# Two Strassen levels instead of one for the last 1024 tokens' products with w_out

## The chip, the cores and the metric

The kernel runs on one core of a Trainium2 chip. The metric is device time in microseconds (us); lower is better. Engines are named as in the profile: PE (matmuls), PEld (weight loads for PE), DVE (vector), ACT (scalar), POOL (GpSimd), SP (its queue issues DMAs here). Each engine works off its own instructions in program order, and waits on semaphores for others.

## The reference

A decayed linear attention over 8 batches, 8 heads, 576 tokens, head size 64, and then a feed-forward block without a non-linearity other than a product:

```
ret = (scores * Dmat) @ v          # scores = q k^T / 8, Dmat = gamma^(i-j) for i >= j
x   = ret as [8*576, 512]
a, b = x @ w1, x @ w2              # 512 -> 1024 each
out = ((a * b) @ w3) @ w_out       # 1024 -> 1024 -> 512
```

All data are fp32. The output has 4608 rows of 512.

## The kernel before

**Merged weights.** `(ab @ w3) @ w_out` is computed as `ab @ (w3 @ w_out)`: the product of the two weights is made once (`w3_mm`, L536) and kept as the tile `w3o`, 1024 x 512. "Products with w_out" are products of `ab` (tokens x 1024) with it. `live["W"]` names the seven forms of it that Strassen's algorithm needs, in Winograd's variant: four quarters `B11`, `B21`, `B22`, `T3` (in `w3o`, the last in place of the fourth quarter) and three sums `T1`, `T2`, `-T4` (tile `wB`). A form is 512 x 256: four chunks of 128 rows on partitions, 256 columns.

**Stages.** Batches go in four pairs. The first pair and the first 64 tokens of each other batch go through single-level code (`up`, L585; `down`, L754). For each of the three other pairs (loop over `s`), 1024 tokens remain: 512 of each of two batches. For them the code does

- the attention, in chunks of 128 tokens (`head`, `tail`), between which the `down` calls of the pair before are laid;
- `up2` (L1039): `x @ w1` and `x @ w2` by two levels of Strassen. For each half `h` of the 1024 features there are seven outer products (order `ORDER` = 1, 2, 6, 5, 3, 7, 4), each of seven inner ones (`INNER` = 1, 5, 6, 2, 7, 3, 4): 14 blocks `k` of 7 products, 98 in all, of 256 columns each;
- products of a and b (`multiply`, L1116) in place in `slab`, which leaves `ab` there;
- `down` (L733): products of two tiles of 128 tokens with `w3o`, one Strassen level, seven products of four matmuls with 256 columns; sums on DVE into `ot`, stores to DRAM from ACT's queue (`store`, L812).

For the pairs `s` = 0 and 1 the four `down` calls are laid between the attention chunks of the next pair. For the last pair (`s` = 2) nothing follows, so four `down` calls stand alone at the end. A call takes 12.09 us.

**The order.** It is written out by hand: each engine gets its instructions in the order in which the Python code issues them. In `up2` a product has a slot number, 7k + 2 x (position in `INNER`), so that two neighbouring blocks interleave (odd and even slots). `at_slot(n, fn)` puts further work behind the product of slot n (the dict `side`).

**Banks and evictions in `up2`.** Each block has two PSUM banks of its own, x and y, and a bank `z` is shared. Product 1 goes to x; ACT copies x to z (L1087); product 2 adds onto z; products 6, 7 and 4 add onto x; 5 and 3 onto y. So product 7 may only begin when the eviction of product 6 has read x, product 4 when that of product 7 has, and so on. Evictions are DVE additions from PSUM into `slab` (L1082; 128x512, or "wide" 128x1024 in outer product 7), ACT copies (L1089), or, for products 2 and mostly 4, an ACT copy into a ring of three buffers (L1081) and a POOL addition from it (L1082 on POOL).

**At the start of `up2`** the token sums are made: T3 and T2 on DVE before it, T1 on DVE behind slot 1, and T4 on POOL, issued behind slot 12, all at L1018 (128x1792). `T4` needs T2 alone. The weight forms of `up2` come from DRAM into four buffers `FB` (`fetch`); `TT` holds T2, T4 and T1. POOL does six `multiply` calls, behind slots 27 to 93; DVE does the other two, right after `up2` and inside the first `down`. In the last `up2`, `ahead` puts one DVE sum of the first `down` (`S3`, L713) behind slot 66.

Of the kernel before, what the change touches and what calls it, by code (L numbers as in the profile page):

```python
# [42 lines left out]
def kernel(  # L43
# [80 lines left out]
    def new(nm, shape, tag=None):  # L124

        if "banks" not in pools:
            return acc.tile(shape, F32, tag="acc", name=nm)
        got = tag or free.pop(0)
        t = pools["banks"].tile(shape, F32, tag=got, name=nm)
        if not tag:  # L130
            held[id(t)] = got, t
        return t

    def done_with(t):
        if id(t) in held:
            free.append(held.pop(id(t))[0])
# [589 lines left out]
    def ahead(x, y, n=3):  # L726
        todo_sums = pair_of(x, y)[2]
        for _ in range(min(n, len(todo_sums))):
            aside.append(todo_sums.pop(0))
# [3 lines left out]
    def down(x, y, then=None, last=False, within=None, hold=False, by_ring=False):  # L733
        a, done, left = pair_of(x, y)
        ahead(x, y)
        while len(done) < 3:
            aside.pop(0)()
        if then:
            ahead(*then)
        ps = {}  # L740
        pool, tag = (F_pool, "ring") if by_ring else ot_pool or (pools["ot"], "ot")
        ot = pool.tile([P, 2, 2, DM // 2], F32, tag=tag, name="ot")

        count = [0]

        def hook():
            count[0] += 1
            if within and count[0] in within:
                within[count[0]]()

        def product(nm, A, B, on=None):
            ps[nm] = ps[on] if on else new("po", [P, DM // 2])
            for f in range(NP):
                nc.tensor.matmul(ps[nm], a[A][:, f // 2, f % 2, :], live["W"][B][:, f, :], start=(f == 0 and not on),  # L754
                                 stop=(f == NP - 1), skip_group_check=True)

        def plus(nm, to, sb):
            nc.vector.tensor_add(ot[:, to[0], to[1]], ps[nm], ot[:, sb[0], sb[1]])  # L758
            if nm != 5:
                done_with(ps[nm])  # L760
            if beside:
                beside.pop(0)()

        def put(m, t, row, half=slice(0, 2)):

            for at, n, r in rows(m, t):
                stores.append((out[r:r + n, half.start * DM // 2:half.stop * DM // 2],
                               ot[at:at + n, row, half].rearrange("p h d -> p (h d)")))
            if not keep_stores:
                store()  # L770

        C11, C12, C21, C22 = (0, 0), (0, 1), (1, 0), (1, 1)
        product(1, "A11", "B11")
        nc.scalar.copy(ot[:, 0, 0], ps[1])  # L774
        hook()
        product(7, "S3", "T3")
        hook()
        product(2, "A12", "B21", on=1)
        nc.vector.tensor_tensor(out=a["S4"], in0=a["A12"], in1=a["S2"], op=ALU.subtract)
        hook()  # L780
        product(6, "S2", "T2")
        plus(6, C12, C11)
        hook()
        nc.scalar.copy(ot[:, 0, 0], ps[2])
        done_with(ps[2])
        plus(7, C21, C12)
        product(5, "S1", "T1")
        plus(5, C22, C21)
        hook()
        product(4, "A22", "-T4")  # L790
        plus(4, C21, C21)
        put(*y, 1)
        if last:
            put(*x, 0, slice(0, 1))
        hook()
        product(3, "S4", "B22", on=5)
        while aside:
            aside.pop(0)()
        plus(3, C12, C12)
        if hold:  # L800
            keep_stores.append(True)
        put(*x, 0, slice(1 if last else 0, 2))
        if hold:
            keep_stores.clear()
        hook()
# [233 lines left out]
    def up2(side, n0):  # L1039

        z = new("upz", [P, 2, NS], "z")
        ring = F_pool.tile([P, 3, 2, NS], F32, tag="ring", name="ring")
        begun_at = {}
        moved = {(1, 1): 3, (12, 5): 98, (12, 6): 100}
        late = {(1, 1): 8}
        slots = sorted((moved.get((k, pos), 7 * k + 2 * pos), k, pos) for k in range(14) for pos in range(7))
        waiting = {}

        def one(slot, k, pos):
            h, j, pr = k // 7, ORDER[k % 7], INNER[pos]  # L1050
            a, b = weights(n0 + k, pr), token_form(j)[:, RHS[pr]]
            if pr == 1:
                begun_at.setdefault(k, [None, None])[0] = new("up", [P, 2, NS])
            elif pr == 5:
                begun_at.setdefault(k, [None, None])[1] = new("up", [P, 2, NS])
            x, y = begun_at[k]
            ps = {1: x, 6: x, 7: x, 4: x, 5: y, 3: y, 2: z}[pr]
            for w in range(2):
                nc.tensor.matmul(ps[:, w, :], a[:, w, :], b, start=(pr in (1, 5) and w == 0), stop=True,  # L1059
                                 skip_group_check=True)  # L1060
            src, dst = TARGET[j]
            S = slab[:, h:h + 2]
            wide = j == 7
            if wide:
                out = old = S[:, :, 2:4] if h == 0 else S[:, :, 1:4:2]
            else:
                out = S[:, :, AT[h][dst]]
                old = None if src is None else S[:, :, AT[h][src]]

            def spread(t):  # L1070
                return t.unsqueeze(2).to_broadcast([P, 2, 2, NS]) if wide else t

            def at(t, l):
                return t[:, :, :, l] if wide else t[:, :, l]

            def add(l, first, by_ring=False):
                got, engine = ps, nc.vector
                if by_ring:
                    got, engine = ring[:, turn[0] % 3], nc.gpsimd
                    turn[0] += 1  # L1080
                    nc.scalar.copy(got, ps)  # L1081
                engine.tensor_tensor(out=at(out, l), in0=spread(got), in1=at(old if first and old is not None else out, l),  # L1082
                                     op=ALU.add)

            def evict():
                if pr == 1:
                    nc.scalar.copy(z, x)  # L1087
                elif old is None and pr in (2, 5, 6, 4):
                    nc.scalar.copy(at(out, {2: 0, 5: 3, 6: 1, 4: 2}[pr]), ps)  # L1089
                elif pr in (2, 4):  # L1090
                    add(0 if pr == 2 else 2, True, by_ring=pr == 2 or not (j == 7 or j == 4))
                elif pr in (5, 6):
                    add(3 if pr == 5 else 1, True)
                else:
                    add(3 if pr == 7 else 1, False)
                if pr == 3:
                    done_with(y)
                elif pr == 4:
                    done_with(x)

            if (k, pos) in late:
                waiting[late[k, pos]] = evict
            else:
                evict()
            if slot in waiting:
                waiting.pop(slot)()
            for n in [n for n in side if n <= slot]:
                for fn in side.pop(n):
                    fn()

        for slot, k, pos in slots:
            one(slot, k, pos)

    def multiply(h, c, engine=nc.vector):
        p = AT[h][c]
        return lambda: engine.tensor_tensor(out=slab[:, h, p], in0=slab[:, h, p], in1=slab[:, h + 1, p], op=ALU.mult)  # L1116


    short_v = {}

    def load_two():
# [111 lines left out]
    for s in range(NB2 - 1):  # L1233
# [84 lines left out]
        def at_slot(n, *fns):  # L1318
            side.setdefault(n, []).extend(fns)
# [18 lines left out]
        for h in halves:  # L1338
# [3 lines left out]
            if h == 0:  # L1342
                at_slot(t + 50, multiply(h, 22, nc.gpsimd))
                at_slot(t + 54, multiply(h, 21, nc.gpsimd))
        ahead((m, 4), (m, 5), 1)
        at_slot(66, aside.pop(0))
        up2(side, 14 * s)
        multiply(1, 22)()
        beside.extend([idle, multiply(1, 21)])
    last = [((m, t), (m, t + 1)) for t in (4, 6, 0, 2)]  # L1350
    for e in range(4):
        ot_pool[:] = [F_pool, "F0"] if e % 2 else []
        down(*last[e], last[e + 1] if e < 3 else None, last=e == 3)


# [41 lines left out]
```

## Time and profile before

| what | us |
|---|---|
| median of three runs (818.97 to 820.53) | 820.45 |
| time of the profiled execution | 820.0 |
| its span | 818.3 |
| last `up2`, 98 products of PE | 681.95 to 766.5 |
| four `down` calls on PE | 766.56 to 815.07 |
| last eviction, DVE L758 | 815.11 to 815.53 |
| last store issued by ACT | 815.56 |

The share of busy time of an engine is over the whole span. "128*128 128x256" in a matmul's row means weights of 128 rows by 128 columns, and 256 columns streamed past them. One fp32 matmul of the code shows as two instructions. A matmul's duration includes its way through the pipeline, so the rate is read from starts, not from durations. In timeline rows the first number is the start, the second the length in us, and "x3" says that three neighbours are merged; brackets give the idle time before and who ended it.

### The profile page before, as it was taken

The page shows a single profiled execution, that of the slowest core. Times are in us where ns is not written, and L with a number is a line of the kernel's source. Part 1 is how long each engine was busy: PE and PEld are TensorE (multiplying, and loading weights), DVE is VectorE, ACT ScalarE, POOL GpSimd, SP SyncE. Part 2 cuts the span into 40 slices and gives each one's busy share as a digit, 9 for nine tenths or more (in the row PEclk, how much of TensorE's full clock was granted, in tenths as well). Part 3 has the DMA queues.
Part 4 walks back from the last instruction along what each step waited for, and adds up shares of the span by engine and source line. Part 5 has one row for each costly group of instructions (what it writes and reads, how often), then busy time and mean ns, then how long its engine had stood idle before and what let it go on. Part 6 is the DMA issues. An engine that isn't in the chain of part 4 may idle for free.

```text
span 818.3 us, 14501 instructions
## 1 busy us (share of the span) xinstructions
PE 805.2 (98%) x5679; PEld 696.7 (85%) x5679; DVE 526.5 (64%) x787; ACT 243.3 (30%) x439; POOL 219.6 (27%) x148
## 2 busy tenths in 40 slices
PE   8999999999999999999999999999999999999998
PEld 7888999744788999888888888888888888888887
DVE  4699999997446585766545766555575656455633
ACT  3677546675110112113222111233211112232100
POOL 1110020000100503205657014167541213464300
PEclk9999999999999999999999999999999999999999
DMA  9994355569227966756964775458646612442011
GB/s 180 212 219 126 80 105 140 134 163 312 42 57 117 233 178 172 233 144 160 224 161 137 168 139 116 80 154 225 175 173 126 115 52 71 138 171 98 0 52 52
DMA packets 224036, 115.34 MB, mean 141 GB/s; under 512 B 195672, under 2 KB 207192, under 8 KB 223968
## 3 DMA queue, kind: packets, MB, share of 16 engines
q1 hardware_dynamic: 171584, 93.40, 45.1%
q10 hardware_dynamic: 52384, 21.01, 11.8%
q8 instruction: 45, 0.74, 0.4%
q14 instruction: 23, 0.19, 0.1%
HBM read 92.09 MB, written 22.28 MB: 140 GB/s over the span
## 4 chain that ended last, share of the span: by engine, by line
PE 80%; DVE 9%; DMA 4%; SPq 3%; issue 2%; ACT 1%; POOL 0%; ACTq 0%; DVEq 0%
PE up L1059 27%; PE po L754 23%; PE up L585 9%; PE ps L536 6%; PE upz L1059 4%; PE xps L363 3%; PE sc L294 3%; DMA ld_v<-in_v_dram 2%; PE st L317 1%; PE up L638 1%; DMA bl_q<-in_q_dram 1%; PE xps L336 1%; DVE room L203 1%; DVE room L590 1%; SPq L896 1%
## 5 line engine op out<-in xcount | busy, mean ns | idle before, releaser
L1082 DVE TENSOR_TENSOR room<-up,room 128x512 f32<-128x512 f32 (+1 forms) x168 | 129.1, 784 | 104.4 <-PE up L1059 101.8
L585 PE MATMUL up<-room 128*128 128x192 f32 x808 | 135.5, 328 | 2.0 <-DVE room L590 1.8
L585 PEld LDWEIGHTS up<-room 128*128 128x128 f32 x808 | 131.1, 190 | 5.0 <-DVE room L590 2.6
L754 PE MATMUL po<-w3o,room 128*128 128x256 f32 x544 | 124.1, 382 | 1.5 <-DVE ot L758 1.5
L1059 PE MATMUL up<-room,form 128*128 128x256 f32 x528 | 125.2, 379 | 0.0
L754 PEld LDWEIGHTS po<-w3o,room 128*128 128x128 f32 x544 | 102.0, 190 | 17.7 <-DVE ot L758 2.6
L1059 PE MATMUL up<-room 128*128 128x256 f32 x480 | 114.4, 379 | 0.0
L1059 PEld LDWEIGHTS up<-room,form 128*128 128x128 f32 x528 | 100.3, 190 | 13.6
L1082 POOL TENSOR_TENSOR room<-ring,room 128x512 f32<-128x512 f32 (+1 forms) x60 | 81.7, 1378 | 84.1 <-ACT ring L1081 84.1
L1059 PEld LDWEIGHTS up<-room 128*128 128x128 f32 x480 | 91.2, 190 | 12.4
L265 POOL TENSOR_TENSOR ld_v<-ld_v,gk 128x1024 f32<-128x1024 f32 (+1 forms) x19 | 39.6, 2086 | 227.9 <-DMA ld_v<-in_v_dram 91.7
L758 DVE TENSOR_TENSOR ot<-po,ot 128x256 f32<-128x256 f32 x90 | 37.7, 419 | 49.5 <-PE po L754 48.5
L754 PE MATMUL po<-wB,forms 128*128 128x256 f32 x288 | 67.5, 382 | 0.0
L590 DVE TENSOR_TENSOR room<-up,room 128x384 f32<-128x384 f32 x75 | 41.4, 552 | 33.1 <-PE up L585 32.3
L754 PEld LDWEIGHTS po<-wB,forms 128*128 128x128 f32 x288 | 54.0, 190 | 7.9 <-PE xps L363 0.5
L536 PE MATMUL ps<-wo,w3T 128*128 128x512 f32 x128 | 55.4, 594 | 0.6 <-DVE w3T L489 0.6
L243 POOL TENSOR_TENSOR bl_q<-bl_q,gqs 128x512 f32<-128x512 f32 (+1 forms) x26 | 28.3, 1107 | 94.2 <-DMA bl_q<-in_q_dram 94.2
L536 PEld LDWEIGHTS ps<-wo,w3T 128*128 128x128 f32 x128 | 24.2, 190 | 31.3 <-issue 28.9
L297 DVE TENSOR_TENSOR pm<-sc,mask 128x512 f32<-128x512 f32 (+1 forms) x72 | 42.5, 652 | 4.5 <-PE sc L294 4.5
L1116 POOL TENSOR_TENSOR room<-room 128x1024 f32<-128x1024 f32 x18 | 42.4, 2358 | 1.6 <-DVE room L1082 1.6
L1081 ACT COPY ring<-up 128x512 f32<-128x512 f32 x24 | 14.1, 586 | 89.3 <-PE up L1059 89.3
L774 ACT COPY ot<-po 128x256 f32<-128x256 f32 x18 | 6.7, 372 | 107.7 <-PE po L754 73.9
(110 smaller groups left out, 983.3 us busy)
## 6 DMA issues: line engine op xcount, KB each, us to landing
form<-kept SPq DMA_DIRECT2D x22, 896.0 KB, 5.0
room<-kept SPq DMA_DIRECT2D x20, 896.0 KB, 5.2
raw<-in_moe_w_dram SPq DMA_DIRECT2D x64, 128.0 KB, 3.0
out_dram<-ot ACTq DMA_DIRECT2D x28, 256.0 KB, 2.1
kept<-form SPq DMA_DIRECT2D x8, 896.0 KB, 5.6
bl_q<-in_q_dram SPq DMA_DIRECT2D x216, 32.0 KB, 2.5
ld_v<-in_v_dram ACTq DMA_DIRECT2D x12, 512.0 KB, 7.4
bl_k<-in_k_dram SPq DMA_DIRECT2D x160, 32.0 KB, 2.9
```

The costliest lines, as they stand in the source:

```text
L243: nc.gpsimd.tensor_tensor(out=part, in0=part, in1=gqs[:, :, n0:n0 + n].unsqueeze(3).to_broadcast([P, NP, n, BL]), op=ALU.mult)
L265: engine.tensor_tensor(out=t, in0=t, in1=gam[:sz, c].unsqueeze(1).unsqueeze(3).to_broadcast([sz, 2, H, D]), op=ALU.mult)
L294: nc.tensor.matmul(sc[j][:sz, p, :sz], kT[hs, b, p, :sz], qT[hs, b, p, :sz], start=True, stop=True)
L297: nc.vector.tensor_mul(pm[:sz, b, j, :, :sz], sc[j][:sz, :, :sz], mask[:sz, :sz].unsqueeze(1).to_broadcast([sz, NP, sz]))
L536: nc.tensor.matmul(ps, live["w3T", ft][:, g, :], live["wo"][:, g, :], start=(g == 0), stop=(g == KF - 1))
L585: nc.tensor.matmul(ps[:, w, :], a[:, w, r, :], b[:, r, :], start=(new and w == r == 0), stop=(w == r == 1), skip_group_check=True)
L590: nc.vector.tensor_add(c[:, to], ps, c[:, sb])
L754: nc.tensor.matmul(ps[nm], a[A][:, f // 2, f % 2, :], live["W"][B][:, f, :], start=(f == 0 and not on), stop=(f == NP - 1), skip_group_che ...
L758: nc.vector.tensor_add(ot[:, to[0], to[1]], ps[nm], ot[:, sb[0], sb[1]])
L1059: nc.tensor.matmul(ps[:, w, :], a[:, w, :], b, start=(pr in (1, 5) and w == 0), stop=True, skip_group_check=True)
L1082: engine.tensor_tensor(out=at(out, l), in0=spread(got), in1=at(old if first and old is not None else out, l), op=ALU.add)
L1116: return lambda: engine.tensor_tensor(out=slab[:, h, p], in0=slab[:, h, p], in1=slab[:, h + 1, p], op=ALU.mult)
```

## The change

The four `down` calls at the end are gone. In their place `deep(m)` computes the same 1024 x 1024 by 1024 x 512 product with two levels of Strassen: the outer level splits tokens, features and output columns in two, and the inner one does so again.

- There are seven outer products (`DORDER` = 1, 7, 6, 4, 5, 3, 2) of seven inner ones, with slots, banks, `z` and ring as in `up2`. Each of the 49 products has four matmuls (two halves of 256 tokens, two chunks of features) with 128 columns, L1261. An eviction is 128x256, and wide (128x512) in outer products 6 and 5: DVE L1278, ACT L1282 and L1284, by the ring ACT L1277 and POOL L1278. Results lie in `ot`, now in the room of `TT`, and are stored from SP's queue (`put`, L1247).
- `w_sums(j)`: the inner forms of each of the seven w_out forms, four sums of 128x256 each (L1150), one in place, three into `spare` room in tiles that the attention has left. Forms 1 and 7 on DVE, behind slots 3 to 24 of the last `up2`; the five others on POOL, behind slots 5 to 89.
- `outer_of(j)`: the outer sums of tokens, two of 128x1024 for each of four (DVE, L1175). S3 behind slots 62 and 64 of `up2`, S1 and S2 at the seam, S4 in the new phase.
- `inner_of(j)`: the inner sums of each outer token form, four of 128x512 (DVE, L1211). Those of the first two behind slots 76 to 90 of `up2`, the others in the new phase.

The two earlier pairs are unchanged.

```
-        ahead((m, 4), (m, 5), 1)
-        at_slot(66, aside.pop(0))
+        if nxt:
+            ahead((m, 4), (m, 5), 1)
+            at_slot(66, aside.pop(0))
+            up2(side, 14 * s)
+            multiply(1, 22)()
+            beside.extend([idle, multiply(1, 21)])
+            continue
+        w_sums, outer_of, inner_of, run = deep(m)
...
+        at_slots((3, 6, 9, 12, 15, 18, 21, 24), w_sums(1) + w_sums(7))
+        at_slots((5, 8, 11, 14, 17, 20, 23, 31, 34, 37, 40, 60, 63, 66, 69, 72, 80, 83, 86, 89),
+                 [fn for j in DORDER[2:] for fn in w_sums(j, nc.gpsimd)])
+        at_slots((62, 64), outer_of(7))
+        at_slots((76, 78, 80, 83), inner_of(1))
+        at_slots((84, 86, 88, 90), inner_of(7))
         up2(side, 14 * s)
...
+        S1, S2 = outer_of(5), outer_of(6)
+        S1[0]()
         multiply(1, 22)()
-        beside.extend([idle, multiply(1, 21)])
-    last = [((m, t), (m, t + 1)) for t in (4, 6, 0, 2)]
-    for e in range(4):
-        ot_pool[:] = [F_pool, "F0"] if e % 2 else []
-        down(*last[e], last[e + 1] if e < 3 else None, last=e == 3)
+        at_slots((0, 1, 2), [S1[1]] + S2)
+        at_slots((9, 10, 11, 12, 13), inner_of(6) + [multiply(1, 21)])
+        at_slots((14, 16, 18, 20), inner_of(4))
+        at_slots((22, 23, 24, 25), inner_of(5))
+        at_slots((27, 29, 30, 31, 32, 33), outer_of(3) + inner_of(3))
+        at_slots((36, 37, 38, 39), inner_of(2))
+        run(side)
```

The core of `deep` and `run` (new):

```
+    DORDER = (1, 7, 6, 4, 5, 3, 2)
+    WFORM = {1: "B11", 2: "B21", 3: "B22", 4: "-T4", 5: "T1", 6: "T2", 7: "T3"}
...
+            return [tt(x(0, 1), x(1, 1), x(0, 1)), tt(e(1), x(0, 1), x(0, 0), ALU.add), tt(e(0), x(1, 1), e(1)), end]
...
+            ot = part_of("TT", 0, 4, 2, 2, 2, P)
...
+            slots = sorted((7 * k + 2 * pos, k, pos) for k in range(7) for pos in range(7))
...
+                for q in range(2):
+                    for f in range(2):
+                        nc.tensor.matmul(ps[:, q], a[:, f, q * P:(q + 1) * P], w[:, f],
+                                         start=(pr in (1, 5) and q == f == 0), stop=(f == 1), skip_group_check=True)
...
+                if pr == 1:
+                    nc.scalar.copy(z, x)
+                elif old is None and pr in (2, 5, 6, 4):
+                    nc.scalar.copy(of(to, {2: 0, 5: 3, 6: 1, 4: 2}[pr]), ps)
+                elif pr in (2, 4):
+                    add(0 if pr == 2 else 2, True, by_ring=k < 6)
+                elif pr in (5, 6):
+                    add(3 if pr == 5 else 1, True)
+                else:
+                    add(3 if pr == 7 else 1, False)
```

More of the change, by code (lines that the diff above doesn't have):

```diff
@@ L1116, in multiply, with spare @@
         return lambda: engine.tensor_tensor(out=slab[:, h, p], in0=slab[:, h, p], in1=slab[:, h + 1, p], op=ALU.mult)
+    def spare(pool, tag, n, bufs=1):
+        shape = {"ld": [P, 2 * H, D], "pm": [P, 2, 2, NP, P], "sb": [P, 2, NP, D]}.get(
+            pool if pool == "ld" else tag, [P, 2, NP, P])
+        t = pools[pool].tile(shape, F32, tag=tag, name="spare", bufs=bufs)
+        names = " ".join(f"d{k}" for k in range(len(shape) - 1))
+        return t.rearrange(f"p {names} -> p ({names})")[:, :n]
@@ new lines, with deep, w_sums, buf @@
+    DORDER = (1, 7, 6, 4, 5, 3, 2)
+    WFORM = {1: "B11", 2: "B21", 3: "B22", 4: "-T4", 5: "T1", 6: "T2", 7: "T3"}
+    RESULT = {21: 0, 22: 1, 12: 2, 11: 3}
+    def deep(m):
+        w_forms, a_forms = {}, {}
+        def w_sums(j, engine=nc.vector):
+            w = live["W"][WFORM[j]]
+            b = [[w[:, 2 * r:2 * r + 2, c * P:(c + 1) * P] for c in range(2)] for r in range(2)]
+            tag = (["ld_q"] * 3 + ["ld_k", "ld_v", "kT", "qT"])[j - 1]
+            got = []
+            def buf():
+                if not got:
+                    t = spare("ld" if tag[0] == "l" else "fr", tag, 6 * P, 3 if tag == "ld_q" else 1)
+                    got.append(t.rearrange("p (s r c) -> p s r c", s=3, r=2))
+                return got[0]
+            def tt(out, in0, in1, op=ALU.subtract):
+                return lambda: engine.tensor_tensor(out=out(), in0=in0(), in1=in1(), op=op)
+            def x(r, c):
+                return lambda: b[r][c]
+            def e(k):
+                return lambda: buf()[:, k]
+            def named():
+                w_forms[j] = {1: b[0][0], 2: b[1][0], 3: b[1][1], 7: b[0][1], 5: buf()[:, 0], 6: buf()[:, 1], 4: buf()[:, 2]}
+            last_sum = tt(e(2), x(1, 0), e(1))
+            def end():
+                last_sum()
+                named()
+            return [tt(x(0, 1), x(1, 1), x(0, 1)), tt(e(1), x(0, 1), x(0, 0), ALU.add), tt(e(0), x(1, 1), e(1)), end]
+        slabs = [slab[:, h].rearrange("p c l s -> p c (l s)") for h in range(2)]
+        A11, A21 = slabs[0][:, 0:4:2], slabs[0][:, 1:4:2]
+        A12, A22 = slabs[1][:, 0:2], slabs[1][:, 2:4]
+        free2 = slab[:, 2].rearrange("p (s c) l x -> p s c (l x)", s=2)
+        def outer(out, in0, in1, op, k):
+            return lambda: nc.vector.tensor_tensor(out=out()[:, k], in0=in0()[:, k], in1=in1()[:, k], op=op)
+        S3 = []
+        def s3_place():
+            if not S3:
+                S3.append(spare("fr", "pm", 16 * P).rearrange("p (c x) -> p c x", c=2))
+            return S3[0]
+        forms = {1: lambda: A11, 7: s3_place, 6: lambda: free2[:, 1], 4: lambda: A22, 5: lambda: A21,
+                 3: lambda: free2[:, 0], 2: lambda: A12}
+        def outer_of(j):
+            to = forms[j]
+            in0, in1, op = {7: (1, 5, ALU.subtract), 5: (5, 4, ALU.add), 6: (5, 1, ALU.subtract),
+                            3: (2, 6, ALU.subtract)}[j]
+            return [outer(to, forms[in0], forms[in1], op, k) for k in range(2)]
+        def inner_of(j, place):
+            n = 4 * P
+            got = []
+            def places():
+                if not got:
+                    got.extend(t.rearrange("p (f x) -> p f x", f=2) for t in place())
+                return got
+            def x(b, k):
+                return forms[j]()[:, k].rearrange("p (f b x) -> p f b x", f=2, b=2)[:, :, b]
+            def s3():
+                return places()[3] if len(places()) > 3 else x(1, 0)
+            def tt(out, in0, in1, op=ALU.subtract):
+                return lambda: nc.vector.tensor_tensor(out=out(), in0=in0(), in1=in1(), op=op)
+            def s(k):
+                return lambda: places()[k]
+            def end():
+                tt(s(2), lambda: x(0, 1), s(1))()
+                a_forms[j] = {1: x(0, 0), 2: x(0, 1), 4: x(1, 1), 5: places()[0], 6: places()[1], 3: places()[2], 7: s3()}
+            return [tt(s3, lambda: x(0, 0), lambda: x(1, 0)), tt(s(1), lambda: x(1, 1), s3),
+                    tt(s(0), s(1), lambda: x(0, 0), ALU.add), end]
+        def cut(t, n=3):
+            return [t[:, k * 4 * P:(k + 1) * 4 * P] for k in range(n)]
+        def room_for(k):
+            return [part_of("TT", k * 4 * P, 4 * P)]
+        place = {1: lambda: room_for(0) + room_for(1) + cut(FB[2], 1) + [spare("fr", "sb", 4 * P)],
+                 7: lambda: cut(FB[2])[1:] + cut(FB[3], 1), 6: lambda: cut(FB[0]) + room_for(8),
+                 4: lambda: cut(FB[1]), 5: lambda: cut(FB[2]), 3: lambda: cut(FB[3]), 2: lambda: cut(FB[0])}
+        def run(side):
+            z = new("dz", [P, 2, P], "z")
+            ring = F_pool.tile([P, 3, 2, NS], F32, tag="ring", name="ring").rearrange(
+                "p t a b -> p t (a b)").rearrange("p t (l q x) -> p t l q x", l=2, q=2)[:, :, 0]
+            ot = part_of("TT", 0, 4, 2, 2, 2, P)
+            begun_at = {}
+            slots = sorted((7 * k + 2 * pos, k, pos) for k in range(7) for pos in range(7))
+            def put(dst, b):
+                n, c = {11: (0, 0), 12: (0, 1), 21: (1, 0), 22: (1, 1)}[dst]
+                for q in range(2):
+                    r = (2 * (m - len(small) + 1) + b) * S + starts[1 + 2 * n + q]
+                    nc.sync.dma_start(out[r:r + P, c * 2 * P:(c + 1) * 2 * P],
+                                      ot[:, RESULT[dst], q, b].rearrange("p c x -> p (c x)"))
+            def one(slot, k, pos):
+                j, pr = DORDER[k], INNER[pos]
+                a, w = a_forms[j][pr], w_forms[j][pr]
+                if pr == 1:
+                    begun_at[k] = [new("dn", [P, 2, P]), None]
+                elif pr == 5:
+                    begun_at[k][1] = new("dn", [P, 2, P])
+                x, y = begun_at[k]
+                ps = {1: x, 6: x, 7: x, 4: x, 5: y, 3: y, 2: z}[pr]
+                for q in range(2):
+                    for f in range(2):
+                        nc.tensor.matmul(ps[:, q], a[:, f, q * P:(q + 1) * P], w[:, f],
+                                         start=(pr in (1, 5) and q == f == 0), stop=(f == 1), skip_group_check=True)
+                at = {1: 3, 7: 1, 4: 0, 3: 2, 2: 3}.get(j)
+                wide = at is None
+                to = ot[:, 1:3] if wide else ot[:, at]
+                old = {1: None, 7: ot[:, 3], 6: ot[:, 1:4:2], 4: ot[:, 1]}.get(j, to)
+                def of(t, l):
+                    b, c = divmod(l, 2)
+                    return t[:, :, :, b, c] if wide else t[:, :, b, c]
+                def add(l, first, by_ring=False):
+                    got, engine = ps, nc.vector
+                    if by_ring:
+                        got, engine = ring[:, turn[0] % 3], nc.gpsimd
+                        turn[0] += 1
+                        nc.scalar.copy(got, ps)
+                    engine.tensor_tensor(out=of(to, l), in0=got.unsqueeze(1).to_broadcast([P, 2, 2, P]) if wide else got,
+                                         in1=of(old if first and old is not None else to, l), op=ALU.add)
+                if pr == 1:
+                    nc.scalar.copy(z, x)
[7 more added lines that the diff above has]
+                    add(3 if pr == 7 else 1, False)
+                if pr == 3:
+                    done_with(y)
+                elif pr == 4:
+                    done_with(x)
+                done = {4: (21,), 5: (22,), 3: (12,), 2: (11,)}.get(j, ())
+                for dst in done:
+                    if k < 6 and pr == 4:
+                        put(dst, 0)
+                        put(dst, 1)
+                    elif k == 6 and pr in (3, 4):
+                        put(dst, int(pr == 4))
+                for n in [n for n in side if n <= slot]:
+                    for fn in side.pop(n):
+                        fn()
+            for slot, k, pos in slots:
+                one(slot, k, pos)
+        return w_sums, outer_of, lambda j: inner_of(j, place[j]), run
@@ L1344, with at_slots @@
                 at_slot(t + 54, multiply(h, 21, nc.gpsimd))
-        ahead((m, 4), (m, 5), 1)
-        at_slot(66, aside.pop(0))
-        up2(side, 14 * s)
-        multiply(1, 22)()
-        beside.extend([idle, multiply(1, 21)])
-    last = [((m, t), (m, t + 1)) for t in (4, 6, 0, 2)]
-    for e in range(4):
-        ot_pool[:] = [F_pool, "F0"] if e % 2 else []
-        down(*last[e], last[e + 1] if e < 3 else None, last=e == 3)
+        if nxt:
[6 more added lines that the diff above has]
+        w_sums, outer_of, inner_of, run = deep(m)
+        def at_slots(slots, fns):
+            assert len(slots) == len(fns)
+            for n, fn in zip(slots, fns):
+                at_slot(n, fn)
+        at_slots((3, 6, 9, 12, 15, 18, 21, 24), w_sums(1) + w_sums(7))
[4 more added lines that the diff above has]
+        at_slots((84, 86, 88, 90), inner_of(7))
+        up2(side, 14 * s)
+        for fns in side.values():
+            for fn in fns:
+                fn()
+        side = {}
+        S1, S2 = outer_of(5), outer_of(6)
+        S1[0]()
+        multiply(1, 22)()
+        at_slots((0, 1, 2), [S1[1]] + S2)
[5 more added lines that the diff above has]
+        run(side)
 _INS = ['q', 'k', 'v', 'moe_w1', 'moe_w2', 'moe_w3', 'moe_w_out']
```

## The prediction

> **What bounds the kernel now.** I read the page first: busy shares, then the chain that ended last.
>
> ```profile
> span 818.3 us, 14501 instructions
> ...
> PE 805.2 (98%) x5679; PEld 696.7 (85%) x5679; DVE 526.5 (64%) x787; ACT 243.3 (30%) x439; POOL 219.6 (27%) x148
> ...
> PE 80%; DVE 9%; DMA 4%; SPq 3%; issue 2%; ACT 1%; POOL 0%; ACTq 0%; DVEq 0%
> ```
>
> PE is 98% busy and carries 80% of the chain. Whatever shortens PE's stream counts in full, as long as no other engine makes PE wait. So I looked next at busy time in the three stretches that the change touches: the last `up2` (681 to 766.5), its end (744 to 767.5), and the four `down` calls (766.5 to 815).
>
> ```profile
> 681.00:766.50 85.50, 85.50 (x398) 75.27 (x397) 49.40 (x61) 24.40 (x42) 46.82 (x27) 1.00 0.34 114
> 766.50:815.00 48.50, 48.50 (x226) 42.40 (x224) 21.09 (x38) 2.98 (x8) 0.00 (x0) 1.00 0.09 36
> ...
> 744.00:767.50 23.50, 23.50 (x111) 20.68 (x110) 14.02 (x19) 5.81 (x10) 14.44 (x9) 1.00 0.12 40
> ```
>
> The columns are length, then busy PE, weight loads, DVE, ACT, POOL, then granted clock. PE has no gap in any of them, at full clock (1.00). In the last `up2` DVE is 58% busy and POOL 55%. In the `down` calls POOL does nothing. The third view is the timeline of PE, for the pitch of matmuls (start to start).
>
> ```profile
> 6.59 1.73 PE L185 MATMUL idle<-ident 128*128 128x128 f32 x14
> ...
> 766.56 5.34 PE L754 MATMUL po<-w3o,room 128*128 128x256 f32 x24
> 771.74 3.62 PE L754 MATMUL po<-wB,forms 128*128 128x256 f32 x16
> ```
>
> 24 instructions start in 771.74 - 766.56 = 5.18 us: 0.2158 us for 256 columns (one fp32 matmul of the code is two instructions here). The top row is the nearest to what the change issues: 128 moving columns, each with its own 128x128 weights. (1.73 - 0.275, its last one's own length) / 13 = 0.112 us; single starts in it lie 0.1115 apart.
>
> Last, DVE and POOL where the last `up2` begins, and a place where both work in SBUF.
>
> ```profile
> 682.50 6.13 DVE L1018 TENSOR_TENSOR room<-room 128x1792 f32<-128x1792 f32 x3
> 688.55 2.83 DVE L1082 TENSOR_TENSOR room<-up,room 128x512 f32<-128x512 f32 x4
> ...
> 686.71 5.77 POOL L1018 TENSOR_TENSOR room<-room 128x1792 f32<-128x1792 f32 x1 [20.71 <-DVE room L1018]
> 692.43 1.27 POOL L1082 TENSOR_TENSOR room<-ring,room 128x512 f32<-128x512 f32 x1
> ...
> 663.60 2.40 POOL L265 TENSOR_TENSOR ld_v<-ld_v,gk 128x1024 f32<-128x1024 f32 x1 [10.10 <-DMA ld_v<-in_v_dram]
> 664.28 2.27 DVE L717 TENSOR_TENSOR forms<-room 128x512 f32<-128x512 f32 x1
> ```
>
> L717 alone takes 0.69 us. Here it was issued at 664.28 while POOL's L265 ran to 666.00, and ended at 666.55: it waited for the whole of POOL's instruction, then ran. POOL's T4 sum (L1018) took 5.77 us against 3.97 at 373.2: it waited for DVE's third sum (to 688.63), then ran to 692.48. So a DVE sum with both inputs in SBUF and a POOL instruction exclude each other, and who has waited goes first. DVE evictions from PSUM do not take part: the first four at L1082 ran from 688.55 inside T4. In the kernel before, almost no DVE sum falls beside POOL work. The change adds many.
>
> **The change, part by part.**
>
> 1. PE in the last phase. Removed: 4 calls x 28 matmuls x 2 = 224 instructions at 0.2158 = 48.34 us. Added: 49 products x 4 matmuls x 2 = 392 at 0.1115 = 43.71 us (0.892 a product). Gain 4.6. Ends: the transposes at L279 (128 columns) go at 0.109, gain 5.6; if each weight load (190 ns, L754's row) lay bare, 74.5 us, a loss of 26. I take the row of the same shape.
>
> The Trainium skill ("TensorE: Matmul & The Clock Gate", section Back-to-back issue gap) says that in a stream of weight load and matmul, 128 columns go at about 81 ns where a lone one goes at 56. By that ratio our 0.109 would be 0.158, the phase 61.9 us, and the change a loss of 14 here; the row of 14 above does not bear that out.
>
> 2. The first sums of w_out forms against T4. Two sums (L1150, w_out form of product 1) are emitted at slots 3 and 6, behind DVE's T1 and ahead of the first eviction (product 7 of block 0). POOL's T4 has then waited since 686.71, so it goes first, 688.6 to 692.5. The two sums (0.42 each, as 128x256 at L758; a sum that has waited ends 0.14 sooner after POOL than it takes alone, as L717 did, so the first ends 0.28 after it) end at 693.2, the eviction (0.69) at 693.9. PE's product 4 of block 0 needs that bank. It is the tenth product: 681.95 + 9 x 0.8633 = 689.72. So PE stands from 689.7 to 694.0: 4.3 us. Lower end, if the sums went first: eviction done at 690.05, 0.4 us. I take 4.3, since both rows above show the one who waited going first.
>
> 3. The other sums in the last `up2`. DVE gets 6 more w_out sums (0.42), two outer sums (1.22, L1116's row) and eight inner ones (0.69); POOL gets 20 (0.62, L1137's row of this size: 12.4 us). Until slot 76 both have room (58 and 55%). In 744 to 767.5 DVE goes to 14.0 + 8 x 0.68 = 19.5 of 23.5 us, POOL to 14.4 + 4 x 0.62 = 16.9. The worst place: POOL's multiply is issued at 748.40 (2.35 us), and DVE comes to the second inner sum of form 1 at 748.46, out of block 10's product 7. It waits to 750.75 and ends at 751.3; two evictions (0.61 each, as they follow one another) and the next inner sum, itself behind a POOL w_out sum and an add, end at 753.7, product 6 of block 11 at 754.3. Its bank is wanted at 752.74: 1.7 us. The same again, smaller, for product 6 of block 12, whose evictions are 1.22 long: 0.4. Ends: 0 (DVE is first by 0.06 us) and 5.2 (all eight sums wait for a full mean POOL instruction, 1.6 us, 72% of the time, less the 4.0 us of room). I take 2.1, the order of issue in the trace.
>
> 4. DVE in the new phase. Start-to-start: six outer sums and two multiplies at 1.2, twenty inner sums at 0.65, eight wide evictions at 0.62, twenty narrow at 0.37: 35.0 us of the 43.7, 32.8 of it ahead of the last sum (slot 39). POOL now has 12 ring adds (0.62, wide 1.27: 10 us, 8.7 by then); sums fill 22.6 of DVE's 32.8 us, so an add meets one in 0.69 of cases and holds it for half its length: 3.0. From 767.5, where DVE is done with `up2`, that is 803.3, while PE unhindered is through with slot 39 at 766.7 + 37 x 0.892 = 799.7. DVE may lie some three products (2.7) behind before a bank is missing: 0.9, rounded to 1.0. Ends 0 and 6.6 (every add in full).
>
> 5. The end. Two stores of 128 KB on SP's queue instead of one on ACT's behind the last eviction: one more issue, 0.3 us (0.34 at L812). SP's fetches in front of them are long done; earlier stores lie under PE. PE's order, ACT's copies (256 wide, 0.37 instead of 0.58) and PSUM's seven banks keep the pattern of `up2`, at about its pace (0.892 against 0.863 a product), so I cost them at nothing; what covers them is those 0.89 us. The `S3` sum of `down` that leaves slot 66 (0.68) was idle time of DVE.
>
> Sum: -4.6 + 4.3 + 2.1 + 1.0 + 0.3 = +3.1 us on the profiled execution's own 820.0 (span 818.3), 0.45 under the median of the three runs: 823.1.
>
> **The rivals.**
>
> A, the forecast: sums and POOL exclude each other, PE stands for some 7 us and the gain is eaten. 823.1, its own range 820.8 to 825.5.
>
> B, faster: the evictions are not held up in step 2, because DVE's next sum gets in ahead of T4. For it: DVE issues the next instruction 0.08 us before the last has ended. Against it: POOL's L265 and T4, above. Then -4.6 + 0.4 + 0.3 and some 1 us of steps 3 and 4: 817.1. It decides for faster once steps 2 to 4 cost under 2.7 us together.
>
> C, much slower: DVE becomes the bound of the new phase, step 4 at its upper end instead of 1.0: up to 823.1 + 5.6 = 828.7, in the middle 826.
>
> D, much slower by PE: 128 columns do not hide the weight load. By the bare loads 820.0 + 26 + 7.7 = 854; halfway between the two pitches 838. Against it: the 14 instructions at 0.112. By the page's ratio it would be 820 + 14 and the stalls, about 840.
>
> **How the numbers follow.** A 0.66, B 0.20, C 0.09, D 0.05. 0.2% of 820.45 is 1.6 us, about what a measurement of this kernel tells from no change: faster is under 818.8, slower over 822.1. A lies 0.48 slower, 0.15 within, 0.03 faster; B 0.15 faster, 0.05 within; C and D slower. Together faster 0.18, same 0.20, slower 0.62. The range goes from B's 817.1 less a little, 816.8, to between C's middle and end, 827.0.
>
> **What would show it.** Step 1: PE at L1261 with 0.1115 between starts. Step 2: DVE's first L1150 some 4 us long, begun near 688.5, and PE idle about 4 us before a product at L1059 by DVE L1082. Step 3: long L1211 rows beside POOL's L1116, PE idle near slot 85. Step 4: PE idle at L1261 by DVE L1278 or L1211 between slots 30 and 45. Wrong would be: no PE gap near 690 (B), or L1261 at a pitch over 0.13 (D).

## The result and the profile after

The changed kernel takes 822.88 us (median; 821.42 to 824.91), the kernel before 820.45. The ratio is 1.0032, with a 95% interval of 1.0018 to 1.0047: slower by 0.3%, against a forecast of 823.1. The size came out right, in part by luck: in the sum behind it two terms were too large, and one that it lacked is nearly as large as their excess.

The profiled execution has a span of 823.2 us (818.3 before). First the page: PE's and the other engines' busy time, and the slices of PE and its clock.

```profile
PE 804.9 (98%) x5847; PEld 701.1 (85%) x5847; DVE 559.4 (68%) x823; ACT 247.7 (30%) x452; POOL 248.6 (30%) x178
...
PE   8999999999999999999999999999999998999998
PEclk9999999999999999999999999999999998999999
```

PE's busy time is that of before to 0.3 us, although its new phase is 4.6 us shorter. Something made it up, and in one slice both PE and its granted clock dip. The windows around that slice (length, then busy PE, PEld, DVE, ACT, POOL, then the granted clock):

```profile
691.00:695.20 4.20, 0.24 (x3) 0.01 (x1) 4.13 (x4) 0.00 (x0) 2.80 (x1) 0.91 0.00 0
695.20:702.00 6.80, 6.80 (x18) 5.50 (x19) 2.59 (x6) 1.74 (x3) 2.28 (x3) 0.55 0.38 135
702.00:709.00 7.00, 7.00 (x34) 6.19 (x33) 4.55 (x9) 1.74 (x3) 3.30 (x4) 1.00 0.37 125
```

PE stands for 4 us, and when it goes on, its clock is at about half for 6 us: 18 instructions in 6.8 us, where 7.0 us hold 34 a little later. In finer windows of this trace the clock is at 0.50 from 694.5 to 701.3. The timeline of DVE, POOL and PE at this place:

```profile
683.85 6.13 DVE L1018 TENSOR_TENSOR room<-room 128x1792 f32<-128x1792 f32 x3
689.90 4.18 DVE L1150 TENSOR_TENSOR w3o<-w3o 128x256 f32<-128x256 f32 x1
694.12 0.42 DVE L1150 TENSOR_TENSOR spare<-w3o 128x256 f32<-128x256 f32 x1
694.46 2.01 DVE L1082 TENSOR_TENSOR room<-up,room 128x512 f32<-128x512 f32 x3
...
688.06 5.74 POOL L1018 TENSOR_TENSOR room<-room 128x1792 f32<-128x1792 f32 x1 [10.29 <-DVE room L1018]
...
695.20 2.08 PE L1059 MATMUL up<-room,form 128*128 128x256 f32 x4 [3.96 <-DVE room L1082]
697.06 1.92 PE L1059 MATMUL upz<-room,form 128*128 128x256 f32 x4
698.77 1.92 PE L1059 MATMUL up<-room 128*128 128x256 f32 x4
```

The first sum of a w_out form, 0.42 us of work, takes 4.18 us: it ends 0.28 us after POOL's T4, at 694.08. The evictions start at 694.46, and PE's product 4 of block 0 goes on at 695.20. From there groups of four matmul instructions start 1.7 to 1.9 us apart where 0.86 is usual (0.2158 each). Summed over the starts of the matmuls, this place costs 4.1 us of standing and 3.1 us of slow matmuls.

The new phase itself, on PE's timeline:

```profile
775.63 1.05 PE L1261 MATMUL dn<-w3o,room 128*128 128x128 f32 x8
...
818.50 1.06 PE L1261 MATMUL dn<-spare,room 128*128 128x128 f32 x8
```

384 instructions start in 818.50 - 775.63 = 42.87 us, 0.1116 each, without a gap. The balance of the span: -4.6 (PE's new phase), +4.1, +3.1, +0.5 (two small stops near 767 and 772), +0.35 at the end (3.1 us behind the last eviction instead of 2.8), and +1.35 by which the last `up2` begins later (683.30 instead of 681.95). The last lies in code that is the same in both kernels; 1.0 of it arises near 345 us. Without it the balance is +3.45, in the medians +2.4. The profiled execution is the longest of the seven and has the lowest mean clock (0.994, the others 0.996 to 0.998), so its 3.1 us of slow matmuls are probably more than the others have.

### The profile page after: what moved, and what is told of

The parts are those of the page before. It is cut to its first block, busy times and chain, and to the rows that moved or that the text cites. A ratio compares the mean times of both kernels' runs of the same rounds, so it can differ in the third digit from the quotient of the medians.

```text
span 823.2 us, 14946 instructions
## 1 busy us (share of the span) xinstructions
PE 804.9 (98%) x5847; PEld 701.1 (85%) x5847; DVE 559.4 (68%) x823; ACT 247.7 (30%) x452; POOL 248.6 (30%) x178
## 4 chain that ended last, share of the span: by engine, by line
PE 79%; DVE 12%; SPq 3%; issue 2%; DMA 2%; ACT 1%; POOL 0%; ACTq 0%; DVEq 0%
PE up L1059 24%; PE po L754 20%; PE up L585 9%; PE ps L536 6%; PE dn L1261 5%; PE upz L1059 4%; PE xps L363 3%; PE sc L294 3%; PE st L317 1%; PE up L638 1%; PE xps L336 1%; DVE room L203 1%; DMA ld_v<-in_v_dram 1%; DVE room L1082 1%; DVE room L590 1%
## 5 line engine op out<-in xcount | busy, mean ns | idle before, releaser
L1082 DVE TENSOR_TENSOR room<-up,room 128x512 f32<-128x512 f32 (+1 forms) x168 | 128.7, 783 | 96.8 <-PE up L1059 94.2
L1059 PE MATMUL up<-room,form 128*128 128x256 f32 x528 | 127.3, 383 | 4.0 <-DVE room L1082 4.0
L1082 POOL TENSOR_TENSOR room<-ring,room 128x512 f32<-128x512 f32 (+1 forms) x60 | 83.2, 1400 | 76.8 <-ACT ring L1081 76.8
L754 PE MATMUL po<-w3o,room 128*128 128x256 f32 x416 | 95.8, 384 | 2.0 <-DVE ot L758 2.0
L754 PEld LDWEIGHTS po<-w3o,room 128*128 128x128 f32 x416 | 77.8, 190 | 15.0 <-DVE ot L758 3.5
L758 DVE TENSOR_TENSOR ot<-po,ot 128x256 f32<-128x256 f32 x70 | 29.2, 418 | 36.7 <-PE po L754 35.9
L754 PE MATMUL po<-wB,forms 128*128 128x256 f32 x224 | 53.1, 384 | 0.0
L754 PEld LDWEIGHTS po<-wB,forms 128*128 128x128 f32 x224 | 41.9, 190 | 6.2 <-PE xps L363 0.5
L363 PE MATMUL xps<-pm,ld_v 128*64 128x128 f32 (+1 forms) x576 | 36.0, 278 | 3.2 <-POOL ld_v L265 3.0
```

Source lines behind the costliest of these rows:

```text
L363: nc.tensor.matmul(banks[r][heads[half], b, n, :sz], vs[:sz, b * H + 2 * p + j, :], pm[:sz, b, j, p, :sz], start=(c == 0 and m == 0), stop ...
```

## The experiments

The first five edits test the two parts of the loss: the lock (a DVE sum with both inputs in SBUF and a POOL instruction keep each other waiting) and the clock. The others test what the prediction said of DVE's and POOL's further sums. Each time is a median, beside runs of the kernel before on the same chip. The kernel before took 819.63 to 820.45 us in these sessions, so a difference between two sessions can be off by some tenths.

**The DVE sums of w_out forms later.**

```
-        at_slots((3, 6, 9, 12, 15, 18, 21, 24), w_sums(1) + w_sums(7))
+        at_slots((17, 20, 23, 26, 29, 32, 35, 38), w_sums(1) + w_sums(7))
```

> The changed kernel with the eight DVE sums for the w_out forms of products 1 and 7 moved from slots 3 to 24 to slots 17 to 38 of the last second-level block, so that none is queued between T1 and the first evictions while T4 runs on POOL. Same work, same counts. Theory (a DVE sum and a POOL instruction exclude each other, T4 goes first, PE stands 4.1 us and then runs some 15 matmuls at half clock, 3.1 us): the gap near 690 and the slow matmuls go, PE starts its first product of the new phase about 85 us after the first of the block; time 820.45 - 4.6 (PE) + 0.4 (end) + about 0.5 (other sums) = 816.7, range 815.5 to 818.5, faster than before. Rival (DVE has too much to do in this block, wherever the sums stand): the wait only moves to slots 20 to 45, 821 to 824.

817.12 us against 820.28 before, ratio 0.9967 (0.9955 to 0.9979): the same work, 5.8 us less than the changed kernel, and faster than the kernel before. The timeline of DVE and POOL:

```profile
682.23 6.13 DVE L1018 TENSOR_TENSOR room<-room 128x1792 f32<-128x1792 f32 x3
688.28 2.83 DVE L1082 TENSOR_TENSOR room<-up,room 128x512 f32<-128x512 f32 x4
...
695.45 0.41 DVE L1150 TENSOR_TENSOR w3o<-w3o 128x256 f32<-128x256 f32 x1
...
686.45 5.77 POOL L1018 TENSOR_TENSOR room<-room 128x1792 f32<-128x1792 f32 x1 [10.29 <-DVE room L1018]
```

Four evictions run inside T4 as before the change; one of their inputs (`up`) is in PSUM. The sum of the row takes 0.41 us. PE lost 0.9 us in the rest of this `up2` (0.4 near 710, 0.2 near 759, 0.3 near 764), none in the new phase. So the place of these sums decides the sign of the change, not the amount of DVE work. All eight moved here; the next run shows that two are enough for the loss.

**The kernel before with two such sums.** Nothing else is changed; the sums go to a spare tile.

```
+        if not nxt:
+            for n, slot in enumerate((3, 6)):
+                at_slot(slot, lambda n=n: nc.vector.tensor_tensor(out=t[...], in0=w[:, 2:4, P:2 * P], in1=w[:, 0:2, P:2 * P], ...))
```

> The kernel before with nothing but two extra DVE sums (128x256, both inputs in w3o, into a spare tile that nobody reads) behind slots 3 and 6 of the last second-level block. 0.84 us of DVE work on an engine that is 58% busy there. Theory: they wait for T4, PE stands 4.1 us near 690 and may then run at half clock for up to 3.1 us: 824 to 828, ratio 1.005 to 1.009. Rival (the loss comes from the amount of added work, or from the new last phase): within 0.5 us of before, 820 to 821.

825.96 us, ratio 1.0074 (1.0059 to 1.0089). 0.84 us of work on an engine that is 58% busy in this stretch costs 5.7 us. The view of DVE, POOL and PE:

```profile
689.07 4.52 DVE L1351 TENSOR_TENSOR spare<-w3o 128x256 f32<-128x256 f32 x2
...
687.24 5.73 POOL L1018 TENSOR_TENSOR room<-room 128x1792 f32<-128x1792 f32 x1 [21.44 <-DVE room L1018]
...
694.25 1.66 PE L1059 MATMUL up<-room,form 128*128 128x256 f32 x4 [3.84 <-DVE room L1082]
695.70 1.91 PE L1059 MATMUL upz<-room,form 128*128 128x256 f32 x4
```

The same picture without any of the new phase: 4.0 us of standing, then 1.8 us of slow matmuls in this execution.

**T4 in seven pieces.** The sums stay at slots 3 and 6.

```
+                "T4s": [tt(TT[:, 1, n], tk[:, 0, 1, n], TT[:, 0, n], engine=nc.gpsimd) for n in range(7)]}
...
-        at_slot(12, sums2["T4"])
+        at_slot(12, *([sums2["T4"]] if nxt else sums2["T4s"]))
```

> The changed kernel with POOL's T4 sum of the last second-level block in seven instructions of 128x256 instead of one of 128x1792; DVE's sums stay at slots 3 and 6. Theory (the lock is held for one whole instruction and the one who waited goes next): each of the two DVE sums waits for one piece of 0.62 to 0.73 us, the first eviction ends near 691.1 by the clock of the profile before instead of 693.9, PE stands 1.2 to 1.6 us instead of 4.1, too short for the clock to fall: 4.1 + (0 to 3.1) - 1.4 less than the changed kernel, 817.5 to 820.5. Rival (DVE waits for T4 as a whole, by a semaphore or because POOL keeps the port between its instructions): PE stands for 4 us or more as before, 822 to 824.

817.24 us, ratio 0.9966 (0.9954 to 0.9978), slightly under the range. DVE's and POOL's timeline, and what PE waited for:

```profile
687.89 0.95 DVE L1151 TENSOR_TENSOR w3o<-w3o 128x256 f32<-128x256 f32 x1
688.88 0.83 DVE L1151 TENSOR_TENSOR spare<-w3o 128x256 f32<-128x256 f32 x1
689.63 2.00 DVE L1083 TENSOR_TENSOR room<-up,room 128x512 f32<-128x512 f32 x3
...
686.06 7.42 POOL L1018 TENSOR_TENSOR room<-room 128x256 f32<-128x256 f32 x7 [10.29 <-DVE room L1018]
...
PE up L1060 <- DVE room L1083: 1.1, 1, 1.1
```

Each sum now waits for one piece only (0.95 and 0.83 us instead of 4.18). PE stands 1.1 us, and no matmul behind it is slow. POOL does the same sum in more time (7.42 us with its waits), and from 680 us on the row above is the only wait of PE that the profile lists. So the lock passes between instructions to the one that has waited, and the wait is set by the length of the other engine's instruction: the same 128x256 sum took 4.18 us behind 128x1792 and 0.95 behind 128x256. The Trainium skill ("SBUF — State Buffer", section Who interferes with whom) says that a DVE instruction with two SBUF inputs contends with a GpSimd instruction that reads SBUF, and that this contention is an exclusive lock. The rows above agree, 4.18 us against 0.95.

**PE kept busy while it waits.** 18 fp32 matmuls of the identity in front of product 4 of block 0.

```
+            if n0 == 28 and (k, pos) == (0, 6):
+                for _ in range(18):
+                    nc.tensor.matmul(warm_t[:, :P], ident, ident, start=True, stop=True)
```

> The changed kernel with 18 fp32 matmuls of the identity (36 instructions of 0.1115 = 4.0 us, into an idle bank) put in PE's order right in front of product 4 of block 0 of the last second-level block, where PE stood for 4.1 us. Nothing else waits for them. Theory (the slow matmuls behind the gap come from the clock that falls because PE idles): the place still costs about 4.1 us, but granted clock stays 1.00 behind it and the 15 matmuls at 0.43 us between starts go back to 0.216; in the profile 3.1 us less than the changed kernel, in the median of runs 0 to 3 less, according to how often its clock falls: 820 to 823. Rival (they are slow for another reason, as operands or evictions late): slow starts remain, no gain.

820.17 us, ratio to before 1.0005 (0.9996 to 1.0014): 2.7 us less than the changed kernel. The wait is the same, DVE's first sum takes 4.20 us, yet no matmul behind it is slow. The window over the place has PE busy throughout and a clock of 1.00:

```profile
689.00:698.00 9.00, 9.00 (x60) 8.28 (x59) 7.71 (x10) 1.74 (x3) 4.86 (x3) 1.00 0.26 85
```

So the slow matmuls came from PE's idling, and cost 2.7 us by the medians, 2.2 by the two ratios to the kernel before. What is left (-0.1 us against before) is the change with its clock intact; its terms in the profile after give -4.6 + 4.1 + 0.5 + 0.35 = +0.4.

**Half of that filling.** 9 instead of 18 (`range(9)`).

> The changed kernel with 9 instead of 18 idle fp32 matmuls in front of product 4 of block 0: they fill 2.0 of the 4.1 us for which PE waits there, and leave a gap of some 2.0 us. The wait itself is the same. Theory (the clock falls when PE idles for long, some 3 to 4 us, and not for short gaps): granted clock 1.00 behind the gap, 820.2 as with 18. Rival (any gap of 2 us brings the half clock): a run of starts at 0.43 us behind it, 822 to 823.

821.18 us, ratio 1.0010 (0.9998 to 1.0022), between both expectations, and the profile has what the theory excluded. PE's timeline and the window behind the gap:

```profile
687.63 2.17 PE L1061 MATMUL idle<-ident 128*128 128x128 f32 x18
691.76 1.13 PE L1063 MATMUL up<-room,form 128*128 128x256 f32 x4 [1.96 <-DVE room L1086]
...
693.10:696.50 3.40, 3.40 (x10) 2.69 (x9) 1.19 (x3) 1.42 (x3) 1.48 (x2) 0.50 0.68 245
```

A gap of 2.0 us was enough for the clock to fall, 1.3 us after PE had gone on. The slow matmuls cost this execution 1.7 us. It does not happen each time: in five of the run's twelve executions the mean granted clock of the whole is 1.000, so there it fell nowhere. A median between the two expectations fits that.

Some of the profiles show the same at the beginning of the program, that of the kernel before among them. Its PE timeline and the window behind the gap:

```profile
21.62 3.53 PE L363 MATMUL xps<-pm,ld_v 128*64 128x128 f32 x32 [2.30 <-POOL ld_v L265]
...
21.50:24.80 3.30, 3.17 (x30) 3.18 (x32) 3.23 (x7) 0.00 (x0) 0.07 (x1) 0.50 1.13 202
```

Counted over all eleven profiles: behind eight gaps of 2.0 to 2.4 us the clock fell five times and stayed three times; behind four gaps of 3.0 to 4.0 us it fell each time; behind gaps of 1.5 us and less it never fell. My 3 to 4 us as the length that it takes fell. In the Trainium skill ("TensorE: Matmul & The Clock Gate", Part 1) the clock goes to half after at least one idle window of about 3.4 us, and windows run free of the kernel. The half clock agrees (0.50 in both rows, and starts 0.427 us apart instead of 0.216 in the changed kernel); the length does not, since gaps of 2.0 to 2.4 us did it in five cases. What decides in such a gap was not tested.

**More sums in the new phase.** The run with late sums, plus four DVE sums of 128x512.

```
+        for n, slot in enumerate((26, 28, 34, 35)):
+            at_slot(slot, lambda n=n: nc.vector.tensor_tensor(out=part_of("tk", 512 * n, 512), in0=part_of("tk", 3072, 512),
+                                                              in1=part_of("tk", 4096, 512), op=ALU.add))
```

> The run with late sums (w_out sums at slots 17 to 38) plus four more DVE sums of 128x512 in the new last phase, behind slots 26, 28, 34 and 35, into a part of the room that nobody reads any more: 4 x 0.65 = 2.6 us of DVE work, and up to 1.3 each of waits for POOL's additions. The output is the same. Theory (DVE lies near its limit in the first 40 slots of this phase: the eviction of product 6 of block 5 ended at 802.28 in the run with late sums, and its bank was wanted at 802.94, 0.66 us later): PE then stands 2 to 4 us before slots 36 to 45, 819 to 821. Rival (DVE has room there, as PE shows no wait): 817.1, within 0.5.

818.76 us, ratio 0.9984 (0.9970 to 0.9998), 1.6 us over the run with late sums: just under the range, above the rival. The intervals of the two ratios overlap a little (0.9970 to 0.9979), but PE's timeline has a stop that the run with late sums has not:

```profile
803.84 1.16 PE L1261 MATMUL dn<-wB,room 128*128 128x128 f32 x8 [1.13 <-DVE room L1278]
```

PE stands once, 1.1 us. 2.6 us of DVE work cost 1.6, so by this estimate about 1 us of room was left: without the four sums DVE is near the bound here, but below it. (This profiled execution has a span of 822.3 us because its last `up2` begins late, some 6 us later than in the run with late sums; the edit comes behind that.)

**Sums moved away from POOL on both engines.** DVE's sums into the pauses behind T4; POOL's last eight forward.

```
-        at_slots((3, 6, 9, 12, 15, 18, 21, 24), w_sums(1) + w_sums(7))
+        at_slots((12, 13, 16, 17, 19, 22, 23, 24), w_sums(1) + w_sums(7))
...
-                 ... 40, 60, 63, 66, 69, 72, 80, 83, 86, 89)
+                 ... 40, 56, 57, 58, 59, 60, 61, 63, 66, 72)
```

> The changed kernel with the eight DVE sums of w_out forms at slots 12 to 24, in DVE's pauses between T4's end and the next POOL additions, and POOL's four sums for product 2 moved from slots 80 to 89 to slots 60 to 72 (those for product 3 to 56 to 59), away from DVE's inner sums. Same work. Theory (only overlaps of DVE sums and POOL instructions cost PE time): the 4.1 us and the half clock go as in the run with late sums, and of the 0.9 us that PE still lost there (0.4 near 710, 0.2 near 759, 0.3 near 764) some 0.5 to 0.9 goes too: 816.2 to 816.8, against 817.1. Rival (the 0.9 us comes from the amount of work): 817 or more.

821.76 us, ratio 1.0023 (1.0008 to 1.0039). The expectation missed by 5 us. The timeline of DVE and POOL, and PE's wait:

```profile
757.14 2.74 DVE L1211 TENSOR_TENSOR room<-room,spare 128x512 f32<-128x512 f32 x1
759.80 2.84 DVE L1211 TENSOR_TENSOR room<-spare,room 128x512 f32<-128x512 f32 x1
...
755.75 3.58 POOL L1082 TENSOR_TENSOR room<-ring,room 128x512 f32<-128x512 f32 x2 [3.15 <-ACT ring L1081]
759.28 2.81 POOL L1116 TENSOR_TENSOR room<-room 128x1024 f32<-128x1024 f32 x1
...
PE up L1059 <- DVE room L1082: 4.0, 2, 3.4
```

Without its small sums POOL came to its wide addition (128x1024, the second of the two in the L1082 row) and its multiply, 2.4 us each, just when DVE's inner sums of slots 88 and 90 came up. Each waited for a whole one: 2.74 and 2.84 us, where the changed kernel has 1.05 and 1.21. PE stood 0.6 and 3.4 us, and the clock fell once more (0.50 from 765.1 to 768.4). Less POOL work at this place made a longer wait.

**Only the DVE part of that edit**, POOL's sums back in place, and beside it the run with late sums once more.

> One of the two edits of the run that dodged, alone: DVE's sums of w_out forms at slots 12 to 24, POOL's sums back at their slots of the changed kernel (80 to 89 for product 2). Theory (the 3.5 us before 765 came because POOL, without its small sums there, reached its wide addition and its multiply just when DVE's inner sums of slots 88 and 90 came up, 2.7 and 2.8 us each): no stop there, at most 0.3 us each near 757 and 762, and the 0.4 near 710 of the late run gone too: 816.5 to 817.3. Rival (the slots of DVE's sums are to blame): 821 to 822 again, with a stop of 3 us near 765.

> The run with late sums (slots 17 to 38) once more, as it stands, beside the run with slots 12 to 24 on the same chip. Theory: 817.1 within 0.6, ratio to the kernel before 0.996 to 0.997; 0 to 0.6 us over the other.

816.44 us for the slots 12 to 24 (0.06 under the range), 816.84 for the late ones again; both have the ratio 0.9962 (0.9947 to 0.9976). There is no stop of 3 us near 765, so POOL's move was to blame. The stop near 710 is gone too: PE loses 0.5 us in the whole of this `up2` instead of 0.9. These are the fastest versions, 0.4% under the kernel before; which of the two is faster, 0.4 us cannot tell.

## Why the prediction was right or wrong, step by step

The rows on which steps 3 and 4 turn: two of the changed kernel, and two of the run with late sums.

```profile
756.94 0.68 DVE L1211 TENSOR_TENSOR room<-room,spare 128x512 f32<-128x512 f32 x1
756.97 2.87 POOL L1116 TENSOR_TENSOR room<-room 128x1024 f32<-128x1024 f32 x1
...
801.87 0.41 DVE L1278 TENSOR_TENSOR room<-dn,room 128x256 f32<-128x256 f32 x1
802.05 1.95 PE L1261 MATMUL dn<-w3o,room 128*128 128x128 f32 x16
```

- **Step 1, PE's new phase**: right. 0.1116 us between starts, the gain 4.6 us. The Trainium skill's ratio for weight loads, 14 us the other way, does not hold for this form: 0.1116 where it would have 0.158.
- **Step 2, two sums behind T4**: right in mechanism, place and size. PE stood 4.1 us (4.3 forecast) near 691, and the edit that moves the sums, the one that cuts T4, and the kernel before with two sums alone each show it.
- **What step 2 lacked**: the clock. I let PE stand for 4 us and go on at full speed. It went on at half, which cost 3.1 us in the profile and 2.2 to 2.7 by the run that filled the gap. The prediction put this at nothing without a word, and it is the largest error of the working.
- **Step 3, the other sums in the last `up2`**: right in kind, too large: 0.5 us instead of 2.1. I had POOL's multiply in front of the second inner sum by 0.06 us. In the profile after, DVE's sum was issued at 756.94 and POOL's multiply at 756.97, so DVE went first and the 1.7 us did not come. I took a tie of some hundredths for an order, and read it wrongly: I had DVE come at 748.46, when the instruction before it ends. But DVE issues the next one 0.08 us earlier, as I say myself under B, so 748.38, ahead of POOL's 748.40. The run that moved POOL's sums shows what the other outcomes cost.
- **Step 4, DVE in the new phase**: too large, 0 instead of 1.0. The count of work was right (the last sum ended at 803.73 in the run with late sums, PE was through with slot 39 at 800.26: 3.5 us behind, 3.6 forecast). But I set the lag of the last sum against the 2.7 us for which PE can go on. What PE waits for is the eviction in front of that sum (the third row above). It ended at 802.28, 2.0 us behind, and its bank was wanted by the second product of the fourth row, at 802.05 + 0.89 = 802.94. The four extra sums confirm a margin of that order.
- **Step 5, the end**: right, 0.35 us.
- **Sum**: +3.1 forecast, +2.4 in the medians. Steps 3 and 4 were 2.6 us too dear, and the clock, worth some 2.5, was missing. That these two cancel is luck: with the clock intact (the run with 18 matmuls) the change measures -0.1, where the working, which knows no clock, has +3.1.
- **Rivals**: B's number, 817.1, is what the kernel takes when its sums do not wait for the whole of T4 (816.4 to 817.2 in four runs). C and D did not occur.

## What to carry to other kernels

Before sums are laid on a vector engine with time to spare, look at which of them have both inputs in SBUF, and at the longest POOL instruction that can run at that moment: that is what such a sum, and everything queued behind it, may wait for. Keep evictions out from behind such sums, or cut the long POOL instruction. And a stop of PE of some microseconds can cost more than its length, since its clock may fall; here 4.1 us became almost 7.

## What was not expected of the hardware

- PE's granted clock fell to half after PE had idled 4.0, 3.4 and 2.0 us in the middle of a busy kernel, and stayed there for 3.4 us, in the changed kernel's profile for 6.8. After gaps of 2.0 to 2.4 us it fell in five cases of eight; after 1.5 us and less it did not fall in the profiles here.
- Cutting one POOL instruction of 128x1792 into seven of 128x256 lengthened the sum from 5.77 to 7.42 us with its waits, and made the kernel 5.6 us faster.
- Taking small POOL instructions out of the way of DVE sums made these wait longer (2.74 and 2.84 us instead of 1.05 and 1.21), since larger ones took their place.
